# Gradient of a gated mix of attention and S4 convolution: early loads between the stages, another memory layout in the S4 loop, and the parameter gradients moved ahead of the last weight-gradient sweep

## The chip, the cores and the metric

The kernel runs on one core of a Trainium2 chip. The metric is the device time of one execution in microseconds (us), taken as the median over several runs. TensorE (PE) multiplies matrices, VectorE (DVE), ScalarE (ACT) and GpSimd (POOL) work on tiles, and SyncE (SP) issues most of the transfers (DMAs). SP, ACT and POOL each feed a DMA queue of their own, and all queues are served by the core's 16 DMA engines. Each engine runs its instructions in the order in which they are written into its program, and an instruction that waits holds up those behind it.

## What is computed

The kernel returns the output and all parameter gradients of this function, for a given gradient of the output:

```python
g = sigmoid((x * gate_w).sum(-1, keepdims=True))
a = attention(x, wqkv, wo)              # 32 heads of 18, S = 2048, D = 576
b = s4_conv(x, A, B, C, log_dt, Dskip)  # 576 channels, 128 states each
out = g * a + (1 - g) * b
...
out, vjp = jax.vjp(f, x, wqkv, wo, A_re, A_im, B_re, B_im, C_re, C_im, log_dt, Dskip, gate_w)
grads = vjp(grad_out)
```

The S4 kernel is K[d, l] = Re sum over n of C[d, n] · exp(dt[d]·A[d, n]·l) · dt[d]·B[d, n]. The convolution of every channel with its K, and the gradients through it, are computed in blocks of 128 positions: within a block by a Toeplitz matrix, and between the 16 blocks by a scan over states.

## The kernel before, in words

All work is in one function, `build`, in four stages.

**First stage** (to about 193 us). The projections, the gate and the S4 parameters are computed and written to HBM: `QKV_d`, `dO_d`, `par_d`, and reordered copies of x and of the output gradient (`xb_d`, `gyb_d`, `xr_d`, `gyr_d`).

**Attention, forward and backward** (to about 2190 us). The work of every four heads and 512 queries is a unit of 32 steps, and the backward rows follow the forward rows by `OFF` = 39 steps, so that ACT's two kinds of exponentials (`PT`, L799, and `eb`, L804), DVE's `ds` (L809) and PE's products interleave. The order on all five engines is written out by hand. After the last forward step (`NTOT`) a tail of 39 steps has only backward work, from about 2106 to 2178 us. On the way PE transposes some tiles into a PSUM tile `turn_p`, and DVE copies them out (L563: `dsT`, `dOaT`). The sums of dv and dk are kept in f32 accumulators; the last addition writes a bf16 tile `gb` (L612, L649), which a DMA transpose turns into `gT` (L532), POOL packs (`dtk`) and a DMA writes to `dqkv_d`. Beside this POOL computes the basis `E_d` of the S4 stage.

**S4 stage** (to about 2726 us), 18 blocks of 32 channels, in these steps for a block b:

- `m_load`: loads `xs` (1 MB) and `gyp`; `m_part`: products `psM` on PE, copied by ACT to `mst` and written to `Md_d`; `m_skw`: read back from `Md_d` along diagonals (`skw`); `m_sum` and `m_fin`: summed on PE (`misc`) and put into `RX`.
- `load_en`: loads the basis in two halves `E1n` of 1 MB; `turn_e`: PE transposes them (`etp`), ACT copies them out as `E1e`.
- `load_rx`, `prep_rx`: loads `RXn` for two blocks, and makes `RX` of it with three ACT operations.
- `uv`: products of `E1e` and `RX` on PE (`uvp`), copied by ACT to `UV`.
- `scan`: 15 dependent steps on DVE over `HG`, the first of which is a copy (L993) that marks the start of a block below. `casts`, `rw1`, `rw2`: the scan's results for PE (`hR`, `gR`, `Rw`).
- `k0`: one column of K into `Kp_d`; `t0_load`: the Toeplitz tile `T0w` (1 MB) out of it; `t0` and `ybp`: products into `yp`, copied to `yd` and every second block written to `yd_d`.
- `pairs1`, `pairs2`, `sums`: products on DVE, summed on PE into `SS` for the parameter gradients.

The order on PE, ACT, DVE and POOL is that of the program text; only SP's order is chosen by the scheduler. A lead-in brings blocks 0 to 2 on their way, and the loop runs block i together with uv of block i+1 and the m steps and loads of blocks i+2 and i+3:

```python
                m_load(0)
                load_rx(0)
                load_en(0, 0)
                load_par(0)
                load_en(0, 1)
                m_load(1)
                m_part(0, 0)
...
                for i in range(-1, NBLK):
```

**Final stage.** `x_tok`, then four column ranges of the token gradients (`load_dq(0)` to `load_dq(3)` into `dq_all`) are loaded, and between them the parameters (`zz`, `Wri`, `dt_b`, `prm5`). PE makes dWqkv in 20 groups of 16 matmuls (`ps_dwq`: four column ranges `FQS`, five row chunks each). DVE computes the parameter gradients in a chain (L1202 and around) that ends in six tiles `opad`; PE transposes each (`opt`, L1278), ACT copies (`obo`, L1280), and POOL issues the output DMAs (L1281, L1283). Two short products `fr` give the gradient of log_dt. Then a loop over 16 token tiles makes the two outputs of token shape (`ps_a`, `ps_dx`), with the transposed tiles `OT4` (L1342, per four tiles) and `dqT` (L1352, each tile) and `y_b`, `dxr_b` from `yd_d`. `pgw` and `ps_dwo` come last.

Memory comes from pools that open and close with the stages. By default, the first use of memory that an earlier pool had waits for everything that used the earlier pool there. With `reuse_waits="tile"` it waits for the users of those tiles alone that lay at the same addresses.

Of the kernel before, what the change touches and what calls it, by code (L numbers as in the profile page):

```python
# [20 lines left out]
def build(tc, aps, dbg_aps=None, stages=("s1", "attn", "post", "s4", "final")):  # L21
# [40 lines left out]
    with ExitStack() as gctx:  # L62
# [366 lines left out]
        if "attn" in stages:  # L429
# [5 lines left out]
            with ExitStack() as ctx:  # L435
                ctx.enter_context(tc.manual_schedule(engines={mybir.EngineType.PE, mybir.EngineType.Activation, mybir.EngineType.DVE, mybir.EngineType.Pool, mybir.EngineType.SP}))
                ga = ctx.enter_context(tc.tile_pool(name="ga", bufs=2))
                ptp = ctx.enter_context(tc.tile_pool(name="ptp", bufs=41))
                work = ctx.enter_context(tc.tile_pool(name="awork", bufs=2))
                apsp = ctx.enter_context(tc.tile_pool(name="aps", bufs=1, space=bass.MemoryType.PSUM))  # L440
# [85 lines left out]
                def grad_tile():  # L526
                    return work.tile([P, KB], BF, tag="gb", bufs=2, name="gb")

                def store_grad(gb, g, which, t0):
                    c0 = which * D + g * 4 * DH  # L530
                    gT = work.tile([P, TPQ, 4, HP], BF, tag="gT", bufs=2, name="gT")
# [21 lines left out]
                def turn(tiles, outs):  # L553
# [6 lines left out]
                    def ev():  # L560
                        x = 0
                        for n, o_ in outs:
                            nc.vector.tensor_copy(o_(), pt_[:, x:x + n])  # L563
                            x += n
# [32 lines left out]
                def dv_half(g, b, kq, h, acc):  # L597
# [6 lines left out]
                    def ev():  # L604
# [5 lines left out]
                        if b == NQ - 1:  # L610
                            o_ = DKV[("v", g, kq)] = grad_tile()
# [21 lines left out]
                def dk_half(g, b, kq, h, acc):  # L633
# [7 lines left out]
                    def ev():  # L641
# [5 lines left out]
                        if b == NQ - 1:  # L647
                            o_ = DKV[("k", g, kq)] = grad_tile()
# [179 lines left out]
        if "s4" in stages:  # L828
# [3 lines left out]
            s4c_cm = tc.tile_pool(name="s4c", bufs=1)  # L832
# [7 lines left out]
            with ExitStack() as ctx:  # L840
                pc = ctx.enter_context(tc.tile_pool(name="s4l", bufs=1))
                pw = ctx.enter_context(tc.tile_pool(name="s4lw", bufs=1))
                pps = ctx.enter_context(tc.tile_pool(name="s4lps", bufs=1, space=bass.MemoryType.PSUM))
# [13 lines left out]
                for u in range(2):  # L857
                    g_u = pc.tile([P, 2 * SUB, CB], BF, name=f"gyp{u}")
                    nc.vector.memset(g_u[:, SUB:2 * SUB, :], 0.0)
                    gyp2.append(g_u)  # L860
# [18 lines left out]
                def load_rx(xb):  # L879
                    d0 = xb * XB  # L880
                    RXn = pw.tile([P, 2 * NB, XB], BF, tag="RXn", bufs=1, name="RXn")
                    nc.sync.dma_start(RXn[:, 0:NB, :], xr_d[:, :, d0:d0 + XB])
                    nc.sync.dma_start(RXn[:, NB:2 * NB, :], gyr_d[:, :, d0:d0 + XB])
                    RXs[xb] = [RXn, None]
# [14 lines left out]
                def m_load(b):  # L899
                    xs = xss[b] = pw.tile([P, NSUB, SUB, CB], BF, tag="xs", bufs=2, name="xs")  # L900
                    src = bass.AP(tensor=xb_d.tensor, offset=xb_d[b:b + 1, 0:1, 0:1].offset,
                                  ap=[[XR * SUB * CB, NB], [SUB * CB, NSUB], [1, NSUB * SUB * CB]])
                    nc.sync.dma_start(xs.rearrange("p e t c -> p (e t c)"), src)
                    nc.sync.dma_start(gyp2[b % 2][:, 0:SUB, :].rearrange("p t c -> p (t c)"), gyb_d[b])
# [19 lines left out]
                def m_skw(b):  # L924
                    skw = skws[b] = pw.tile([P, CB // 8, P], F32, tag="skw", name="skw")
# [24 lines left out]
                def turn_e(b, h, q0, q1):  # L950

                    B_ = blk(b)
                    if q0 == 0:
                        B_["E"][h] = pw.tile([P, GS, 2, N], BF, tag="E1e", bufs=2, name="E1e")
                    En, E_ = B_["En"][h], B_["E"][h]
                    for q in range(q0, q1):
# [4 lines left out]
                        nc.scalar.copy(E_[:, 4 * q:4 * q + 4], pt_)  # L961

                def load_par(b):
                    par = blk(b)["par"] = pw.tile([P, 12, CB], F32, tag="par", bufs=2, name="par")
                    nc.sync.dma_start(par, par_d[:, 0:12, b * CB:(b + 1) * CB])

                def load_en(b, h):
                    dG = b * CB + h * GS
                    En = blk(b)["En"][h] = pw.tile([P, GS, 2, P], BF, tag="E1n", bufs=6, name="E1n")
                    nc.sync.dma_start(En, E_d[:, dG:dG + GS])  # L970
# [80 lines left out]
                def ybp(b, h):  # L1051
# [12 lines left out]
                    if h == 1 and b % 2 == 1:  # L1064
                        x0 = (b // 2) * XB
                        nc.sync.dma_start(yd_d.rearrange("p a b d -> p (a b) d")[:, :, x0:x0 + XB], yd.rearrange("p a b d -> p (a b) d"))
# [48 lines left out]

                m_load(0)
                load_rx(0)
                load_en(0, 0)
                load_par(0)
                load_en(0, 1)  # L1120
                m_load(1)
                m_part(0, 0)
                m_part(0, 1)
                m_skw(0)
                turn_e(0, 0, 0, 2)
                prep_rx(0)
                turn_e(0, 0, 2, 4)
                m_sum(0)
                m_fin(0)
                k0(0)  # L1130
                t0_load(0)
                load_en(1, 0)
                load_en(1, 1)
                load_en(2, 0)
                load_en(2, 1)
                m_part(1, 0)
                m_part(1, 1)
                for i in range(-1, NBLK):
                    cur = i >= 0
# [3 lines left out]
                    if sb is not None:  # L1143
# [21 lines left out]
                    if sb is not None:  # L1165
                        prep_rx(sb)
                    if cur:
# [21 lines left out]
        if "final" in stages and "s4" in stages:  # L1189
# [14 lines left out]
            with ExitStack() as ctx:  # L1204
                pb = ctx.enter_context(tc.tile_pool(name="pb", bufs=1))
                pps = ctx.enter_context(tc.tile_pool(name="pps", bufs=2, space=bass.MemoryType.PSUM))
                pbw = ctx.enter_context(tc.tile_pool(name="pbw", bufs=2))
# [14 lines left out]
                with ExitStack() as actx:  # L1222
                    pf = actx.enter_context(tc.tile_pool(name="pf", bufs=1))
# [220 lines left out]
```

## Time and profile before

| | us |
|---|---|
| median of three runs | 2948.57 (2947.92 to 2948.86) |
| span of the profiled execution | 2936.2 |
| attention, first PE product to last | 203 to 2184 |
| first scan of the S4 stage, block 0 / block 1 / block 2 | 2234.66 / 2262.93 / 2289.82 |
| last product of the loop on PE | 2724.0 |
| `ps_dwq` | 2741.05 to 2805.2 |
| token loop, from the first `ps_a` | 2824.37 to 2908.8 |
| `pgw` and `ps_dwo` | 2908.8 to 2932.6 |

The page gives the busy share of each engine in 40 slices of the span. A windows view gives for a stretch of time the busy microseconds and, in brackets, the number of instructions of each engine, then the clock that PE was granted, the busy share of the DMA engines, and what they moved. A timeline gives the start and duration of each instruction, its engine and line, what it writes and reads, and in square brackets how long its engine had been idle and what released it. SPq and ACTq are the issues of DMAs by these engines.

### The profile page before, as it was taken

To read this page: it belongs to the slowest core of one execution; us is meant where nothing else is said; L and a number is where in the kernel's file an instruction comes from. 1 tells how busy PE (TensorE), PEld (TensorE's weight loads), DVE (VectorE), ACT (ScalarE), POOL (GpSimd) and SP (SyncE) were. 2 spreads that over 40 slices of the span, in tenths; PEclk is the share of its full clock that TensorE was granted. 3 is DMA by queue.
4 is the path that set the end of the run, shared out by engine and by line. 5 is a ranking of instruction groups with operands and counts; after the bars stand their busy time and mean duration, and the time that the engine had idled before them with its cause. 6 is when DMAs were issued, how large, how long until landed. Compare 5 with 4: busy or idle time off the path is not lost.

```text
span 2936.2 us, 69578 instructions
## 1 busy us (share of the span) xinstructions
PE 2460.4 (84%) x27132; PEld 1182.8 (40%) x27132; DVE 2357.5 (80%) x4147; ACT 2375.9 (81%) x2792; POOL 1606.4 (55%) x2653
## 2 busy tenths in 40 slices
PE   4768988988888898898898888888866888885779
PEld 2432333332333233233333323333225878885457
DVE  4445998898898899799899989889864999999634
ACT  2449999999999999899999989999836877785111
POOL 1028888888788788787888778878210000000010
PEclk8877999999999999899999999999977888888889
DMA  8855899999989989988998998998789888882985
GB/s 224 163 152 106 157 157 171 158 164 160 170 153 167 170 153 168 168 150 161 164 168 152 166 157 156 161 173 146 130 141 263 216 222 228 214 221 63 268 195 131
DMA packets 1293343, 499.99 MB, mean 170 GB/s; under 512 B 1187774, under 2 KB 1263136, under 8 KB 1283796
## 3 DMA queue, kind: packets, MB, share of 16 engines
q1 hardware_dynamic: 1264500, 434.91, 77.1%
q0 software_dynamic: 20624, 53.26, 7.4%
q10 hardware_dynamic: 7888, 7.38, 0.8%
q8 instruction: 212, 3.47, 0.5%
q14 instruction: 119, 0.97, 0.1%
HBM read 144.48 MB, written 99.69 MB: 83 GB/s over the span
## 4 chain that ended last, share of the span: by engine, by line
ACT 34%; DVE 24%; PE 21%; DMA 8%; issue 7%; POOL 4%; SPq 3%; ACTq 0%; DVEq 0%; POOLq 0%
ACT eb L804 20%; ACT PT L799 13%; PE ps_P L30 7%; DVE ds L809 7%; DVE tz L999 4%; DVE tz L1002 3%; DVE HG L1003 2%; PE accV L30 2%; PE turn_p L558 2%; PE ps_dx L30 2%; DMA gT<-gb 2%; PE ps_dwq L30 2%; PE accK L30 2%; DVE pq L1069 1%; POOL et L358 1%
## 5 line engine op out<-in xcount | busy, mean ns | idle before, releaser
L809 DVE TENSOR_TENSOR ds<-ps_P,PT 128x512 bf16<-128x512 f32 x2048 | 1310.5, 682 | 123.2 <-PE ps_P L30 82.5
L804 ACT ACTIVATE eb<-ps_P 128x1024 bf16<-128x1024 f32 x1024 | 1098.7, 1073 | 72.1 <-PE ps_P L30 71.0
L799 ACT ACTIVATE PT<-ps_P 128x1024 bf16<-128x1024 f32 x1024 | 1102.0, 1079 | 3.2 <-PE ps_P L30 2.3
L30 PE MATMUL ps_P<-dOaT,VaT_g 32*128 32x512 bf16 x2048 | 580.6, 389 | 31.2 <-DVE ds L809 16.1
L358 POOL TENSOR_TENSOR et<-eG,eT 128x448 f32<-128x448 f32 x576 | 542.1, 961 | 10.7
L30 PE MATMUL ps_P<-QaT_g,KaT_g 32*128 32x512 bf16 x2048 | 412.9, 395 | 145.2 <-ACT PT L799 129.5
L30 PE MATMUL ps_P<-KaT_g,QaT_g 32*128 32x512 bf16 x2048 | 407.5, 391 | 2.2 <-ACT eb L804 1.6
L30 PEld LDWEIGHTS <-KaT_g 32*128 32x128 bf16 x2048 | 147.2, 91 | 480.1 <-issue 465.5
L358 POOL TENSOR_TENSOR Eo<-et,et 128x448 bf16<-128x448 f32 x288 | 327.0, 1136 | 20.8
L1105 POOL TENSOR_TENSOR SS<-m 128x96 f32<-128x96 f32 x18 | 8.9, 497 | 518.3 <-ACT m L1103 518.3
L30 PEld LDWEIGHTS <-QaT_g 32*128 32x128 bf16 x2048 | 115.9, 91 | 286.7 <-issue 265.1
L30 PE MATMUL accO<-PT,Vtok_g 128*32 128x512 bf16 x2048 | 213.2, 403 | 0.0
L30 PE MATMUL accV<-eb,dOa 128*32 128x512 bf16 x2048 | 184.6, 394 | 28.3 <-ACT eb L804 28.3
L30 PE MATMUL accK<-dsT,Qtok_g 128*32 128x256 bf16 x4096 | 166.6, 285 | 4.0 <-DMA dsT<-ds 2.4
L558 PE MATMUL turn_p<-ident_bf,ds 128*128 128x128 bf16 x1664 | 137.3, 226 | 32.1 <-DVE gb L630 31.2
L30 PE MATMUL accQ<-ds,Ktok_g 128*32 128x512 bf16 x2048 | 159.4, 389 | 2.5 <-DVE gb L612 2.1
L961 ACT COPY E1e<-etp 128x1024 bf16<-128x1024 bf16 x144 | 135.7, 1037 | 23.3 <-PE etp L960 17.7
L563 DVE COPY dsT<-turn_p 128x1024 bf16<-128x1024 bf16 (+1 forms) x224 | 143.7, 641 | 3.8 <-PE turn_p L558 3.8
L30 PEld LDWEIGHTS <-Vtok_g 128*32 128x32 bf16 x2048 | 53.6, 93 | 224.9 <-issue 224.1
L558 PEld LDWEIGHTS <-ds 128*128 128x128 bf16 x1664 | 100.4, 100 | 80.4 <-issue 80.4
L30 PEld LDWEIGHTS <-E1n 128*128 128x128 bf16 x2304 | 96.7, 109 | 87.2 <-issue 86.8
L30 PE MATMUL yp<-Rw,E1n 128*128 128x30 bf16 x1152 | 67.7, 232 | 68.7 <-DVE Rw L1024 54.2
(247 smaller groups left out, 3710.1 us busy)
## 6 DMA issues: line engine op xcount, KB each, us to landing
E_d<-Eo POOLq DMA_DIRECT2D x144, 256.0 KB, 3.7
E1n<-E_d SPq DMA_DIRECT2D x36, 1024.0 KB
xs<-xb_d SPq DMA_DIRECT2D x18, 1024.0 KB
T0w<-Kp_d SPq DMA_DIRECT2D x18, 1024.0 KB
Md_d<-mst SPq DMA_DIRECT2D x36, 288.0 KB
dsT<-ds SPq DMA_TRANSPOSE x512
dqkv_d<-dtk POOLq DMA_DIRECT2D x96, 72.0 KB, 4.4
QKV_d<-stg SPq DMA_DIRECT2D x12, 504.0 KB
```

The costliest lines, as they stand in the source:

```text
L30: return nc.tensor.matmul(out, lhsT=lhsT, rhs=rhs, start=start, stop=stop, **kw)
L358: nc.gpsimd.tensor_tensor(out, a, b, op=op)
L558: nc.tensor.transpose(pt_[:, x, qb, :], t_[:, qb * P:(qb + 1) * P], ident_bf)
L563: nc.vector.tensor_copy(o_(), pt_[:, x:x + n])
L799: nc.scalar.activation(U["PT"][i, j // 2], ps, ACT.Exp)
L804: nc.scalar.activation(e, ps, ACT.Exp)
L809: nc.vector.tensor_tensor(U["ds"][i][:, j, :], ps, U["PT"][i, j // 2][:, j % 2, :], op=A.mult)
L961: nc.scalar.copy(E_[:, 4 * q:4 * q + 4], pt_)
L999: nc.vector.tensor_tensor(tz, HG[:, :, k - 1, :].unsqueeze(1).to_broadcast([P, 2, 4, CB]), ZZ, op=A.mult)
L1002: nc.vector.tensor_tensor(t0v, t0v, UVk[:, :, :, k, :], op=A.add)
L1003: nc.vector.tensor_tensor(HG[:, :, k, :].rearrange("p (r s) c -> p r s c", s=2), t0v, t1v[:, ::-1], op=A.add)
L1069: nc.vector.tensor_tensor(o.rearrange("p a b n c -> p a b (n c)"), a_.rearrange("p b n c -> p b (n c)").unsqueeze(1).to_broadcast([P, 2, 2 ...
```

## The change

- **Pools.** The pools of attention, S4 stage and final stage get `reuse_waits="tile"`. The loop's tiles are spread over more pools in another order (`pl_` for the loads, `ple` for `E1n`, `pw` for the rest), so that they lie at other addresses.
- **Attention.** The last dv and dk sums are written as bf16 into the accumulators themselves, so that `gb` needs one buffer, and `gT` has three. In the steps from `NTOT` to `NTOT + OFF` the copies out of `turn_p` are made by ACT instead of DVE.
- **Lead-in.** It is written anew, with SP's order fixed too. The loads of block 0 (`xs`, `gyp`, first `E1n`, `RXn`, `par`) are issued by ACT. The `E1e` copies of block 0 are made by DVE. `m_part` of block 2 and its `m_skw` move from the lead-in into the loop's first pass.
- **End of the loop.** The last `yd_d` write is issued by ACT.
- **Final stage.** The first three of the four `ps_dwq` sweeps stand ahead of the parameter gradients as before; the fourth stands behind them.

```diff
-                ga = ctx.enter_context(tc.tile_pool(name="ga", bufs=2))
+                ga = ctx.enter_context(tc.tile_pool(name="ga", reuse_waits="tile", bufs=2))
...
-                            nc.vector.tensor_copy(o_(), pt_[:, x:x + n])
+                            (nc.scalar.copy if NTOT <= now[0] < NTOT + OFF else nc.vector.tensor_copy)(o_(), pt_[:, x:x + n])
...
-                            o_ = DKV[("v", g, kq)] = grad_tile()
+                            o_ = DKV[("v", g, kq)] = in_place(a_)
...
-                pc = ctx.enter_context(tc.tile_pool(name="s4l", bufs=1))
-                pw = ctx.enter_context(tc.tile_pool(name="s4lw", bufs=1))
+                pc = ctx.enter_context(tc.tile_pool(name="s4l", reuse_waits="tile", bufs=1))
+                pl_ = ctx.enter_context(tc.tile_pool(name="s4ld", reuse_waits="tile", bufs=1))
+                ple = ctx.enter_context(tc.tile_pool(name="s4le", reuse_waits="tile", bufs=1))
+                pw = ctx.enter_context(tc.tile_pool(name="s4lw", reuse_waits="tile", bufs=1))
...
-                        nc.sync.dma_start(yd_d.rearrange(...
+                        (act_dma if b == NBLK - 1 else nc.sync.dma_start)(yd_d.rearrange(...
...
-                m_load(0)
-                load_rx(0)
-                load_en(0, 0)
-                load_par(0)
-                load_en(0, 1)
-                m_load(1)
-                m_part(0, 0)
...
-                for i in range(-1, NBLK):
+                with tc.manual_schedule(engines={mybir.EngineType.SP}):
+                    m_load(0, act_dma)
+                    load_en(0, 0, act_dma)
+                    load_rx(0, act_dma)
+                    load_par(0, act_dma)
+                    m_part(0, 0)
+                    m_part(0, 1)
+                    m_skw(0)
+                    load_en(0, 1)
+                    prep_rx(0)
+                    turn_e(0, 0, 0, 4, dve_copy)
+                    m_load(1)
+                    m_sum(0)
+                    m_fin(0)
+                    load_en(1, 0)
+                    uv(0, 0)
+                    turn_e(0, 1, 0, 4, dve_copy)
+                    uv(0, 1)
+                    k0(0)
+                    load_par(1)
+                    prep_rx(1)
+                    m_part(1, 0)
+                    m_part(1, 1)
+                    load_en(1, 1)
+                    t0_load(0)
+                    m_skw(1)
+                    turn_e(1, 0, 0, 4)
+                    m_load(2)
+                    m_sum(1)
+                    m_fin(1)
+                    load_en(2, 0)
+                    load_en(2, 1)
+                for i in range(NBLK):
...
+                    if i == 0:
+                        m_part(2, 0)
+                        m_part(2, 1)
+                        m_skw(2)
...
-                pb = ctx.enter_context(tc.tile_pool(name="pb", bufs=1))
+                pb = ctx.enter_context(tc.tile_pool(name="pb", reuse_waits="tile", bufs=1))
...
-                    for f0, fn, c0 in FQS:
+                    def dwq(f0, fn, c0):
...
+                    for q in FQS[0:3]:
+                        dwq(*q)
...
+                    dwq(*FQS[3])
```

## The prediction

> **What bounds the kernel now.** I read the page first, for where no engine is full, then windows, then the timeline of the places found. All times are from one profiled execution of 2936.2 us.
>
> ```profile
> DVE  4445998898898899799899989889864999999634
> ...
> DMA  8855899999989989988998998998789888882985
> GB/s 224 163 152 106 157 157 171 158 164 160 170 153 167 170 153 168 168 150 161 164 168 152 166 157 156 161 173 146 130 141 263 216 222 228 214 221 63 268 195 131
> ```
>
> A slice is 73.4 us. Attention fills the slices up to about 2178 us and the S4 loop those from 2235 to 2721. Between them lies one slice in which DVE is at 4 tenths, and where the loop ends one in which traffic falls to 63 GB/s. Windows around these places (PE, PE weight loads, DVE, ACT, POOL busy; clock; DMA share; GB/s):
>
> ```profile
> 2200.00:2260.00 60.00, 35.66 (x554) 31.59 (x555) 22.16 (x49) 36.15 (x54) 0.00 (x0) 0.70 0.99 254
> 2500.00:2580.00 80.00, 70.32 (x1164) 66.72 (x1164) 74.97 (x157) 62.63 (x95) 2.78 (x6) 0.87 0.86 219
> 2660.00:2716.00 56.00, 28.46 (x512) 27.72 (x512) 52.61 (x107) 25.04 (x40) 1.94 (x4) 0.77 0.14 33
> 2716.00:2741.00 25.00, 7.26 (x122) 7.19 (x122) 6.33 (x8) 1.65 (x3) 4.52 (x12) 0.64 0.71 209
> 2806.00:2829.00 23.00, 6.22 (x35) 3.49 (x35) 3.48 (x6) 3.76 (x6) 8.59 (x13) 0.58 0.53 128
> ```
>
> Inside the loop DVE is the bound (74.97 of 80). In the lead-in the DMA engines are (0.99), with every compute engine idle part of the time. Just before the loop ends they rest (0.14), and then PE works 7 of 25 us waiting for them. At 2806 nobody is busy: small dependent steps. The timeline names the waits (start, duration, instruction, idle time before it and its releaser):
>
> ```profile
> 2192.35 0.58 SPq L903 DMA_DIRECT2D xs<-xb_d  x1
> ...
> 2199.98 2.10 PE L30 MATMUL psM<-xs,gyp 128*32 128x128 bf16 x32 [15.72 <-DMA xs<-xb_d]
> ...
> 2203.78 2.94 SPq L917 DMA_DIRECT2D Md_d<-mst  x2
> ...
> 2234.66 0.23 DVE L993 CAST HG<-UV 128x128 f32<-128x128 bf16 x1 [48.88 <-DMA Md_d<-mst]
> ...
> 2726.82 9.25 SPq L1228 DMA_DIRECT2D dq_all<-dqkv_d  x2
> ...
> 2741.05 13.77 PE L30 MATMUL ps_dwq<-dq_all,x_tok_b 128*128 128x426 bf16 x64 [17.03 <-DMA dq_all<-dqkv_d]
> ...
> 2746.50 0.76 DVE L1202 TENSOR_TENSOR fta<-zz,SS 128x576 f32<-128x576 f32 x1 [18.79 <-DMA zz<-par_d]
> ...
> 2824.37 2.56 PE L30 MATMUL ps_a<-wo_sb,OT 128*128 128x288 bf16 x10 [8.64 <-DMA OT<-O_tok]
> ```
>
> Each "idle before" is a stage start held by a load, and each load was issued only after the whole stage before had let go of its memory.
>
> **The skill.** "DMA: Bandwidth & Descriptors", section "Queues, rings and completion order": SP and ACT each own one row of rings on the same 16 engines, and an engine alternates between rows that have work. So a load issued by ACT needn't stand behind SP's and shares bandwidth with them. The page of before has 434.91 MB on SP's queue and only 7.38 on ACT's, so it can't confirm this. Its section "Why small descriptors are slow (HBM only)" agrees with the last yd_d write: 512 KB in 128-byte pieces took 5.28 us, 99 GB/s against the lead-in's 254. "TensorE: Matmul & The Clock Gate", Part 1, has an idle array fall to half clock; the trace agrees (0.50 in 2178 to 2200), so a shorter idle stretch saves some slow matmuls too. I count that at nothing, as these stretches still hold waits.
>
> **The change, part by part.** The orders and waits come from the built programs of both kernels; durations from the trace of before.
>
> A, attention's start. The last write of the first stage is issued at 190.89 and the first KaT load, which waits for it, at 193.23. With waits by tile it waits for older writes only: 193.23 − 191.34 (that issue's end) = 1.9 of which I take 1.8 (0 to 2.3). POOL's basis work starts earlier too, off the path.
>
> B, attention's tail, 2108 to 2178. DVE is busy 62.59 of 70 us, ACT 38.78. Nine turn copies (0.41 to 0.69 us on DVE, sum about 5) move to ACT, where a 1024-wide copy takes 1.04. PE, in order, waits both for exps (ACT) and for ds (DVE); a copy ahead of an exp delays it. Between −2 and +4, I take +1.5. In-place dv and dk sums cost nothing: the same DVE operation writes elsewhere.
>
> C, lead-in. xs, gyp, E1n, RXn and par of block 0 go to ACT's queue right after the last exp (2175.39 + 1.02) and wait by tile. ACT has nothing else until 2201, so six issues (0.4 to 0.6 each, one longer) delay nobody but these. xs can start at 2176.5 instead of 2192.35, and psM follows the last accK matmul (2184.3) instead of 2199.98. From psM to the Md_d write was 3.8 us: 2188. That write took 12.72 us to land, behind loads in its own queue; now SP's queue is empty ahead of it, and I take 3 to 5: 2192. Then as in before: skw 2.7, m_sum 2.4, casts about 1: 2198. The two uv halves follow without k0 and psM(1) between (1.84 + 2.17 before), paced by E1n(0,1), 1 MB issued at about 2195 and landed at about 2200, its turn (2 on PE) and UV copies (2.2): the first scan at about 2209 (2207 to 2212), 25 earlier than 2234.66. DVE's eight E1e copies, 8 × 0.69 (its 1024-wide copy at 2181.61), lie in its idle time.
>
> But the gain that counts is that of block 1, since blocks follow at 26.95 us (2289.82 − 2262.93, and the same between later ones). Block 1's earliest is 2209 + 27 = 2236. Its own chain: k0(0) ends about 2209, psM(1) 2211, mst behind three RX casts of block 1 on ACT (4.1) 2215; Md(1) shares the queue with E1n(1,1) and T0w, 2 MB, so about 10 to land: 2225; skw 2.7, m_sum 2.4, cast 1, k0 1.84, uv 2, E1e copies on ACT 3.8, second uv and UV copies 4.2: 2243, plus the hR casts' share of ACT, 2245 (2237 to 2251). Before it was 2262.9: gain 18 (12 to 25). Loads needed by then are about 10 MB, 39 us at 254 GB/s from 2176.5: 2216, so bandwidth alone isn't last. Blocks 2 and on keep their order.
>
> D, end of loop. x_tok (2304 KB) now waits for tiles that block 16's work lets go and is issued some 40 us earlier, into the stretch with DMA share 0.14: free. dq_all(0) still waits for block 17's last yp matmul (2716.75 + 3.56 = 2720.3), so the layout gives it no block, only the 6.5 us from 2720.3 to 2726.82. Its 1708 KB with yd_d's 512 KB need 8.5 us at 266 GB/s (the rate of 2741 to 2806), plus issue and landing about 1.7: ps_dwq at 2730.5 instead of 2741.05. Gain 10.5 (9 to 13). yd_d on ACT's queue removes its 0.56 us issue on SP from in front.
>
> E, final stage. Three of four ps_dwq sweeps (240 matmuls) take 64.1 − 80 × 0.187 = 49.2: 2779.7. Meanwhile DVE's parameter chain starts when zz lands: zz stays behind dq_all(1) on SP, 6.9 earlier than 2746.50, so 2739.6, and its 40.6 us (2746.50 to 2787.09) end at 2780.2. It is thus ready just as PE reaches the 30 opt transposes, which now lie between matmuls of the last sweep: 80 × 0.187 = 15.0 plus 3.5 of transposes and fr gives 2798.2; the waits for output DMAs (2806 to 2818 before) are filled by matmuls, I add 0.3 (up to 3). SP's queue ahead of OT4 (wqkvT, O_tok, go_all, rowb) ended at 2789.5 before and moves earlier with dq_all, so OT4, dxr and dqT, no longer held by the last POOL output, are there at about 2798: ps_a at 2798.5 instead of 2824.34, 25.8, of which D is 10.5 and E 15.3. PE waited for dqT 1.40 and 7.11 us after that; with loads further ahead I credit 2 (0 to 4). The rest (16 tiles, pgw, ps_dwo: 111.9 us) is unchanged. E: 17.3 (13 to 22).
>
> Sum: 1.8 + 1.5 + 18 + 10.5 + 17.3 = 49.1; span 2887. The timed median stands 12.4 above the profile's span, so 2948.57 − 49 = **2900**. Ends summed: 32 and 66.
>
> **Rivals.**
> 1. Lead-in traffic becomes the wait. Its window already had share 0.99; if Md(1) needs the 12.7 us that Md(0) took, and E1n(2,·) and T0w get in front, block 1 starts at 2251 or later: C gives 12 or less. For it: 0.99. Against: loads start 16 us earlier. With some of E lost too: 2908 to 2919.
> 2. Final loads hold ps_a. O_tok and go_all (2304 KB each) and wqkvT stand on SP's queue behind dq_all(2), ahead of OT4, and the share was already 0.91 in 2741 to 2806. If the SP queue keeps its old times, E is about 4, not 17: 2913.
> 3. Everything lands first: block 1 follows block 0 at once (2236, C 26), D 13, E 20: 62, so 2886.
> 4. Slower: the loop's period grows. Block 2's m_part sits inside block 0 and the load pools are rearranged, so traffic may mix with small pieces as in the last stage (2829 to 2909: share 1.00 at 217 GB/s). A block moves 26.95 × 219 = 5.9 MB; at 254 GB/s that is 23.2 us, hidden below DVE's 26.95. Below 219 DMA sets the period, and from 29.7 us (5.9 MB at 199 GB/s) 18 blocks take back the 49: slower beyond. Against it: the same transfers as before.
> 5. It doesn't do what it says: dq_all(0) indeed isn't freed a block early, priced in D already; the other parts don't depend on it.
>
> **Chances.** Forecast 0.60 (gain 38 to 58, so 2890 to 2911), rival 1 0.18, rival 2 0.06, rival 3 0.11, rival 4 0.03, no difference 0.02. The range for 8 in 10 reaches into 1, 2 and 3: 2884 to 2918. About 0.2% (5.9 us) can be told from no change: faster 0.95, same 0.02, slower 0.03.
>
> **What would show it.** Right: psM within 2 us of the last accK; the first scan near 2207, block 1 some 35 us later, then 26.95 each; x_tok issued before the loop's end, dq_all at its last yp; ps_dwq 10 us after; ps_a right behind the last sweep. Wrong: Md(0) again over 10 us in flight; a period above 27; PE idle ahead of opt or ps_a by more than 3 us; more than 2 us lost in attention's tail.

## The result, and the profile after

The changed kernel takes 2912.52 us (median of four runs, 2908.25 to 2918.88) against 2948.24 of before (four runs): a ratio of 0.9884, with a 95% interval of 0.9863 to 0.9904. That is 35.7 us less. The forecast was 49 less, with a range of 31 to 65. A second series gave 2913.64 and a ratio of 0.9882 (0.9854 to 0.9910). The profile fell on the longest of the first four executions (2918.88, span 2917.2), that of the kernel before on a short one (2937.9, span 2936.2), so stages are compared below by their own lengths, and over several profiles where there are some.

The page of the changed kernel, busy tenths in slices of 72.9 us:

```profile
DVE  4445998899898899899999989989865899999744
...
DMA  8764889999999989988998998998789888885795
GB/s 223 165 163 97 157 160 169 158 160 167 160 160 164 175 153 164 174 152 159 168 173 154 165 161 155 160 179 149 132 138 218 219 221 219 228 218 152 189 257 120
```

The slice of the lead-in has DVE at 5 tenths instead of 4, and the one with 63 GB/s at the loop's end is gone: 152 now. The windows show how far each place was mended (columns as before: PE, PE weight loads, DVE, ACT, POOL; clock; DMA share; GB/s):

```profile
2174.00:2214.00 40.00, 18.91 (x225) 14.63 (x224) 8.04 (x18) 9.29 (x15) 4.97 (x12) 0.64 1.01 190
2214.00:2253.00 39.00, 22.59 (x376) 20.41 (x375) 25.07 (x52) 20.78 (x33) 0.00 (x0) 0.69 0.92 224
2253.00:2290.00 37.00, 27.11 (x434) 25.31 (x432) 24.99 (x53) 22.58 (x35) 3.02 (x2) 0.82 0.74 201
...
2500.00:2580.00 80.00, 69.56 (x1164) 65.89 (x1164) 75.00 (x156) 62.44 (x94) 2.49 (x6) 0.87 0.84 215
2660.00:2716.00 56.00, 32.04 (x535) 31.29 (x533) 52.61 (x106) 27.33 (x43) 1.67 (x4) 0.74 0.27 77
2716.00:2730.00 14.00, 7.34 (x124) 6.92 (x124) 6.38 (x8) 1.65 (x3) 3.66 (x11) 0.74 0.54 160
```

The loop's steady part is the same (75.00 of 80 on DVE). The end of the loop now carries x_tok (77 GB/s instead of 33), and the gap behind it is 14 us long instead of 25. The first three lines are the surprise. Block 0's first scan comes at 2214.8, block 1's at 2253.01, and block 2's at 2290.46: DVE is busy 25 of 39 us and 25 of 37 in the two blocks that should already run at the loop's pace. The timeline, instruction by instruction (start, duration, and in brackets the idle time of the engine and its releaser):

```profile
2189.35 1.04 PE L30 MATMUL accK<-dsT,Qtok_g 128*32 128x256 bf16 x16 [9.77 <-DMA dsT<-ds]
2190.18 2.18 PE L30 MATMUL psM<-xs,gyp 128*32 128x128 bf16 x32
...
2214.77 0.23 DVE L999 CAST HG<-UV 128x128 f32<-128x128 bf16 x1 [1.61 <-ACT UV L992]
...
2235.47 8.62 SPq L909 DMA_DIRECT2D xs<-xb_d  x1
2244.14 0.88 SPq L889 DMA_DIRECT2D RXn<-gyr_d  x1
...
2253.01 0.22 DVE L999 CAST HG<-UV 128x128 f32<-128x128 bf16 x1
...
2255.08 2.02 ACT L899 COPY RX<-RXn 128x1024 bf16<-128x1024 bf16 x1 [3.33 <-DMA RXn<-gyr_d]
...
2290.46 0.22 DVE L999 CAST HG<-UV 128x128 f32<-128x128 bf16 x1
...
2679.64 0.44 SPq L1231 DMA_DIRECT2D x_tok_b<-in_A_x_dram  x1
2721.61 2.62 SPq L1250 DMA_DIRECT2D dq_all<-dqkv_d  x2
...
2729.72 31.97 PE L30 MATMUL ps_dwq<-dq_all,x_tok_b 128*128 128x426 bf16 x160 [4.89 <-DMA dq_all<-dqkv_d]
...
2739.62 0.74 DVE L1224 TENSOR_TENSOR fta<-zz,SS 128x576 f32<-128x576 f32 x1
...
2784.71 0.69 ACT L1305 COPY obo<-opt 128x640 bf16<-128x640 bf16 x1 [3.62 <-DMA O_tok<-O_d]
...
2785.45 0.44 PE L1303 MATMUL opt<-ident_bf,opad 128*128 128x128 bf16 x5 [3.12 <-ACT obo L1305]
...
2803.84 1.40 PE L30 MATMUL ps_a<-wo_sb,OT 128*128 128x288 bf16 x10
```

In the kernel before, the last `accK` matmuls ran in one piece:

```profile
2182.36 1.90 PE L30 MATMUL accK<-dsT,Qtok_g 128*32 128x256 bf16 x32 [0.78 <-DVE dsT L563]
```

In the changed kernel the last dsT transpose holds PE for 9.8 us ahead of the last 16 of them. The second half of RXn for blocks 2 and 3 stands behind a load of xs that takes SP 8.6 us to issue, and block 2's RX copies wait for it. The end is as planned: x_tok 42 us ahead of the loop's end, dq_all at its last yp matmul, ps_a right behind the last sweep.

The 19.0 us between the two profiled spans, by stage. "Last accK" is the first of the last 32 accK matmuls, the point at which attention's work on PE ends if nothing is late.

| stage | before | after | difference |
|---|---|---|---|
| start to first attention product | 203.5 | 201.9 | −1.6 |
| first product to last accK | 1978.9 | 1976.7 | −2.2 |
| last accK to first scan of block 0 | 52.3 | 36.2 | −16.1 |
| the same to block 1 | 80.6 | 74.5 | −6.1 |
| **the same to block 2** | 107.5 | 111.9 | **+4.4** |
| first scan of block 2 to that of block 17 | 404.3 | 404.8 | +0.5 |
| first scan of block 17 to ps_dwq | 46.9 | 34.4 | −12.5 |
| ps_dwq to ps_a | 83.3 | 74.1 | −9.2 |
| ps_a to the end | 111.8 | 113.3 | +1.5 |

So in the profiles the new lead-in gains 16 us at block 0 and has lost 4 by block 2, and the gain lies in the end of the loop and the final stage. The second row hides two changes that nearly cancel: the body of attention (first to last forward product) is 10.4 us shorter, 1890.1 instead of 1900.4, and the tail behind it 8.1 longer, 86.6 instead of 78.5.

The medians differ by 36 us where the profiled executions differ by 19: that of before lies about 10 below its median, that of the changed kernel 6 above. Two profiles don't tell which stage makes executions of one kernel differ, so the parts were run alone.

### The profile page after: what moved, and what is told of

Its sections match the earlier page's. It is cut to its first block, busy times and chain, and to the rows that moved or that the text cites. A ratio compares the mean times of both kernels' runs of the same rounds, so it can differ in the third digit from the quotient of the medians.

```text
span 2917.2 us, 69513 instructions
## 1 busy us (share of the span) xinstructions
PE 2484.6 (85%) x27132; PEld 1186.6 (41%) x27132; DVE 2359.3 (81%) x4146; ACT 2377.2 (81%) x2793; POOL 1610.9 (55%) x2653
## 4 chain that ended last, share of the span: by engine, by line
ACT 35%; DVE 23%; PE 23%; DMA 8%; issue 6%; SPq 3%; POOL 0%; ACTq 0%; DVEq 0%; POOLq 0%
ACT eb L808 21%; ACT PT L803 13%; PE ps_P L30 8%; DVE ds L813 7%; DVE tz L1005 3%; PE accV L30 3%; DMA dsT<-ds 2%; DVE tz L1008 2%; DVE HG L1009 2%; PE turn_p L562 2%; PE ps_dx L30 2%; PE accK L30 2%; PE accO L30 1%; DVE pq L1075 1%; DVE dvacc L616 1%
## 5 line engine op out<-in xcount | busy, mean ns | idle before, releaser
L30 PE MATMUL ps_P<-dOaT,VaT_g 32*128 32x512 bf16 x2048 | 587.6, 396 | 28.9 <-DVE ds L813 13.7
L30 PE MATMUL ps_P<-KaT_g,QaT_g 32*128 32x512 bf16 x2048 | 414.3, 397 | 1.2 <-ACT eb L808 0.6
L30 PE MATMUL accV<-eb,dOa 128*32 128x512 bf16 x2048 | 190.5, 405 | 26.6 <-ACT eb L808 25.7
L967 ACT COPY E1e<-etp 128x1024 bf16<-128x1024 bf16 x136 | 128.0, 1034 | 16.5 <-PE etp L966 16.4
L30 PEld LDWEIGHTS <-Qtok_g 128*32 128x32 bf16 x4096 | 88.9, 98 | 97.9 <-issue 64.9
L358 POOL TENSOR_TENSOR et<-eT 128x32 f32<-128x32 f32 (+3 forms) x288 | 116.1, 423 | 11.4
```

The source lines that it names most:

```text
L30: return nc.tensor.matmul(out, lhsT=lhsT, rhs=rhs, start=start, stop=stop, **kw)
L358: nc.gpsimd.tensor_tensor(out, a, b, op=op)
```

## The experiments

Four kernels ran together first, beside the kernel before (2939.45 us in that series). Each series has its own time of the kernel before, so results are compared by their ratio to it.

**The final stage alone.** The kernel before with the change's final stage:

```diff
-                pb = ctx.enter_context(tc.tile_pool(name="pb", bufs=1))
+                pb = ctx.enter_context(tc.tile_pool(name="pb", reuse_waits="tile", bufs=1))
...
+                    for q in FQS[0:3]:
+                        dwq(*q)
...
+                    dwq(*FQS[3])
```

> The kernel before with the final stage of the change alone (waits by tile in its pools, fourth weight-gradient sweep behind the parameter gradients); attention, lead-in and loop as before. My theory now, from the two profiles: the final stage is where nearly all of the measured gain lies (ps_dwq 12.5 us sooner after the last scan, ps_a 9.2 us sooner after ps_dwq, 1.5 us given back in the token loop), so about 20 us less than before, 2928. By the forecast's steps D and E: 27.8 less, 2920. A rival: the early x_tok load needs the loop's new memory layout, which is not in this kernel; then x_tok still goes after the loop and only the sweep's new place counts: 9 to 12 less, 2937.

Measured: 2924.18 us, ratio 0.9952 (0.9931 to 0.9974), 14 us less (7.6 to 20) where my theory had 20 and the forecast 28. In its profile ps_dwq follows block 17's first scan after 44.7 us (before 46.9, changed kernel 34.4), ps_a follows ps_dwq after 72.4 (83.3; 74.1), and the rest takes 107.9 (111.8; 113.3). The rival was right about x_tok, which went out only at 2718.10, behind the loop's last yp matmul: the early loads give 2 of their 12 us. The sweep's new place gives its whole gain without the new layout.

**All but the final stage.** The changed kernel with the final stage of before, its pools and its order:

```diff
-                pb = ctx.enter_context(tc.tile_pool(name="pb", reuse_waits="tile", bufs=1))
+                pb = ctx.enter_context(tc.tile_pool(name="pb", bufs=1))
...
-                    dwq(*FQS[3])
```

> The changed kernel with the final stage of before (pools that wait for the whole stage, parameter gradients behind all four sweeps); attention, lead-in and loop as changed. My theory: the lead-in's 20 us at block 0 are lost again by block 2, and what is left is attention's 3 to 4 us and what differs from execution to execution: 2938 to 2948. By the forecast's steps A, B and C: 21 less than before, 2927.

Measured: 2933.48 us, ratio 0.9986 (0.9967 to 1.0006): steps A, B and C together are not to be told from nothing, where the forecast had 21. My 2938 to 2948 and the forecast's 2927 were reckoned from 2948; against before in the same series the medians differ by 6 and the ratio by 4, which is inside my 0 to 10 and outside the 21 (the interval ends at 9.7). From block 17 to ps_dwq it takes 46.2: with the layout but pools that wait for the whole stage, step D's gain is gone as well. Layout and waits by tile each need the other. (`yd_d` on ACT's queue is in this kernel and not in the one above, so it isn't enough by itself.)

What the new final stage is worth can be read from what this kernel lacks: 0.9986 − 0.9884, or 30 us, give or take 8. Most of the change's 36 us is there.

**Block 0's loads on SP.**

```diff
-                    m_load(0, act_dma)
-                    load_en(0, 0, act_dma)
-                    load_rx(0, act_dma)
-                    load_par(0, act_dma)
+                    m_load(0)
+                    load_en(0, 0)
+                    load_rx(0)
+                    load_par(0)
```

> The changed kernel with block 0's loads issued by SP, behind the last transposes, instead of by ACT. My theory: ACT's loads share the DMA engines with attention's last dsT and gT transposes, and PE waits 9.8 us for dsT ahead of the last accK; here that wait is under 2 us and the last accK ends at about 2181 in the profile, not 2190; psM of block 0 starts within 3 us of where it started in the changed kernel, so the time is 0 to 6 us less, 2906 to 2912. The rival, that transposes were late for another reason: the wait of about 10 us stays, and psM comes 10 or more later: 2912 to 2925.

Measured: 2905.21 us, ratio 0.9891 (0.9871 to 0.9912), the same ratio as the changed kernel's. Its timeline, PE:

```profile
2178.45 1.90 PE L30 MATMUL accK<-dsT,Qtok_g 128*32 128x256 bf16 x32 [0.85 <-DVE dsT L567]
2184.14 2.14 PE L30 MATMUL psM<-xs,gyp 128*32 128x128 bf16 x32 [3.79 <-DMA gyp<-gyb_d]
```

All 32 accK matmuls run in one piece, and psM comes 5.7 us after their start instead of 11.6. So block 0's loads did hold up the transpose, as the Trainium skill would have it in "DMA: Bandwidth & Descriptors", section "Issuing engines are not separate DMA queues": all queues end on the same 16 engines and interleave. The edit changes queue and order at once (on SP the loads stand behind the last dsT), so it doesn't say which of the two counts. Block 0 starts 30.4 us after the last accK instead of 36.2, and psM 6 earlier where I expected 3 or less. But block 2's first scan still comes 110.0 us after the last accK (111.9), and no gain in time shows (the interval of each ratio is 6 us to either side, so a few could hide there). A wait of 10 us was removed on the way to block 0, and little or none of it arrived at block 2: something else sets that.

**Loads in the order of need.**

```diff
                     load_en(1, 0)
+                    load_en(1, 1)
                     uv(0, 0)
...
                     m_part(1, 1)
-                    load_en(1, 1)
+                    m_skw(1)
+                    load_rx(1)
                     t0_load(0)
-                    m_skw(1)
...
-                    if sb is not None and sb % 2 == 0:
+                    if sb is not None and sb % 2 == 0 and i > 0:
                         load_rx(sb // 2)
```

> The changed kernel with the lead-in's loads in the order of need: the second E1n half of block 1 directly behind its first, the read-back of block 1's diagonals ahead of T0w, and RXn of blocks 2 and 3 in the lead-in ahead of xs(2) and E1n of block 2 (in the changed kernel its second half stands behind two xs loads, is issued 23 us after the first half, and ACT waits 3.3 us for it with block 2's chain behind). My theory: block 1's first scan 3 to 6 us earlier and block 2's 5 to 12 earlier than in the changed kernel: 2900 to 2908. The rival, that the 24 MB moved between attention and block 2 set the time whatever their order: within 3 us of 2912.

Measured: 2895.29 us, ratio 0.9854 (0.9832 to 0.9876), about 10 below the 2905 that the changed kernel's ratio gives in this series (0.9884 × 2939.45). The intervals of the two ratios overlap a little, so the time alone would be weak evidence; the profile is not. The second half of RXn is issued 46 us after the last accK (2174.59) instead of 66, block 1's scan comes 63.8 us after it (74.5 in the changed kernel) and block 2's 99.4 (111.9), both earlier than I expected.

```profile
2220.68 1.55 SPq L889 DMA_DIRECT2D RXn<-gyr_d  x1
...
2273.97 0.22 DVE L999 CAST HG<-UV 128x128 f32<-128x128 bf16 x1
```

The wait for dsT is still there (8.15 us). The order of loads on SP was what held block 2, as my theory had it. Which of the three moves counts most was not tried; in the changed kernel's profile the chain to block 2 runs through RXn.

The second series asked about attention, and put the mended parts together (before: 2946.37).

**The changed kernel again.** No edit.

> The changed kernel once more, beside the others of this series. The one profile of it fell on its slowest execution (2918.88 against 2908 to 2913). My theory: attention's length differs from execution to execution by some 10 us in any kernel, and the wait of PE for the last dsT (9.8) and the distance from the last accK to block 2's first scan (111.9, against 107.5 before) are the same every time within 4 us. Ratio to before 0.986 to 0.991. The rival: the profile shows a bad case, and the distance is 100 or less here.

Measured: 0.9882, span 2911.2. The pause inside the last accK is 12.1 us from start to start (10.8 in the first profile), and block 2 comes 117.8 us after the last accK: 5.9 from the first profile, where I expected 4 at most, and away from the rival's 100. In four profiles with the new lead-in (this one, the first, and two more of this section) the distance is 111.9, 117.8, 115.7 and 115.1, in three with the old one 107.5, 108.5 and 110.4. The means are 115.1 and 108.8: the new lead-in costs 6.

**Attention's turn copies back on DVE.**

```diff
-                            (nc.scalar.copy if NTOT <= now[0] < NTOT + OFF else nc.vector.tensor_copy)(o_(), pt_[:, x:x + n])
+                            nc.vector.tensor_copy(o_(), pt_[:, x:x + n])
```

> The changed kernel with the copies out of turn_p in attention's tail back on DVE. In the profiles the tail (last forward product to the first half of the last accK) takes 74 to 79 us with the copies on DVE and 80 to 87 with them on ACT, with PE's granted clock near 1.0 for most of the former and 0.5 for most of the latter. My theory: the copies on ACT cost the tail 7 or so: here it takes 74 to 80 and the time is 4 to 9 us below the changed kernel's in this series. By the forecast's step B the copies on ACT gain 1.5: here 1 to 2 above. A rival, that the clock changes for another reason (waits by tile, in-place sums): tail 84 to 87 here too, and no difference in time.

Measured: 2912.49 us and 0.9882, the changed kernel's ratio to the last digit. My theory fell: the tail took 80.3 us with the copies on DVE and 79.9 with them on ACT in the same series. A small cost of the copies isn't excluded: over the nine profiles with the new attention pools the tail is 83.7 in the mean with the copies on ACT (six: 79.9 to 86.6) and 80.0 with them on DVE (three: 76.9 to 82.9). What remains is that the tail took 74 to 79 us (mean 76.5) in the three kernels with the old attention pools and 77 to 87 (mean 82.5) in those with the new ones, in-place sums alone being among the former, and that long tails go with a clock near 0.5 on PE. Which is cause and which is effect these runs don't say. (A low clock is no sign of idle time there: in 2123.9 to 2133.9 of the kernel before PE was busy 9.91 of 10 us at a granted clock of 0.50.)

**In-place sums alone.** The kernel before, with this only (the third `gT` buffer belongs to it, and was not tried apart):

```diff
-                    return work.tile([P, KB], BF, tag="gb", bufs=2, name="gb")
+                    return work.tile([P, KB], BF, tag="gb", bufs=1, name="gb")
...
-                    gT = work.tile([P, TPQ, 4, HP], BF, tag="gT", bufs=2, name="gT")
+                    gT = work.tile([P, TPQ, 4, HP], BF, tag="gT", bufs=3, name="gT")
...
-                            o_ = DKV[("v", g, kq)] = grad_tile()
+                            o_ = DKV[("v", g, kq)] = in_place(a_)
...
-                            o_ = DKV[("k", g, kq)] = grad_tile()
+                            o_ = DKV[("k", g, kq)] = in_place(a_)
```

> The kernel before with the in-place sums of dv and dk (one gb buffer, three of gT) and nothing else. In the profile of before DVE waits 34.4 us in seven waits for a gT transpose to let go of gb, and PE 30.4 us behind that; in the changed kernel both are gone, and PE waits 20 us for dsT instead of 2.4. My theory: attention's body is 5 to 10 us shorter by this alone, 2939 less 7 if before stands at 2939 again: ratio 0.996 to 0.999. The forecast's step B put it at nothing: 1.000 within 0.001.

Measured: 2933.70 us, ratio 0.9954 (0.9937 to 0.9971), 13.6 us less, more than my theory and far from nothing. The waits view says why. First the kernel before (engine, what waited, for what; us in total, how often, the longest), over attention's body:

```profile
DVE gb L630 <- DMA gT<-gb: 34.4, 7, 7.5
...
PE turn_p L558 <- DVE gb L630: 30.4, 7, 6.9
...
PE accK L30 <- DMA dsT<-ds: 2.4, 3, 1.6
```

At the end of each group of four heads the sums of dq, dk and dv all had to go through two gb buffers, each held by a transpose. DVE stood 34 us in seven waits, and PE 30 us behind it. With the in-place sums alone neither line is in the answer any more, and another has grown:

```profile
PE accK L30 <- DMA dsT<-ds: 20.4, 10, 5.4
```

On the same queue the dsT transposes are late instead; why, these views don't say. The body, first to last forward product, took 1891.6 us instead of 1900.4. The difference to 13.6 is within the interval and within what attention differs between executions.

**The mended parts together.** SP loads, order of need (RXn here behind xs(2) and its gyp), the copies on DVE, and block 2's part moved, with the loads of block 3 behind it:

```diff
                         turn_e(i + 1, 1, 0, 4)
+                    if i == 0:
+                        m_part(2, 0)
+                        m_part(2, 1)
+                        m_skw(2)
+                        m_load(3)
...
-                    if i == 0:
-                        m_part(2, 0)
-                        m_part(2, 1)
-                        m_skw(2)
```

> The changed kernel with what the runs so far point to: block 0's loads on SP behind the last transposes, the lead-in's loads in the order of need, block 2's m_part directly behind the second E1e turn of block 1 (ahead of hR on ACT) with xs(3) behind it, and the copies of attention's tail on DVE. My theory: 0 to 6 for the loads on SP, 10 for the order (measured 2895 against 2905), 6 to 9 for block 2, 4 to 9 for the tail: 17 to 30 below the changed kernel in this series; block 2's first scan 88 to 95 us after the last accK. The rival: traffic bounds the lead-in and one mended wait makes room for the next: no more than the 10 of the order.

Measured: 2889.55 us, ratio 0.9809 (0.9783 to 0.9834), 24 us below the changed kernel beside it, and 57 below the kernel before: the lowest ratio of all. The rival's limit of 10 lies at the edge of what was measured (the two ratios are 21 us apart, 10 to 33). Blocks 0, 1 and 2 start 30.5, 63.8 and 97.5 us after the last accK. The total came as expected, but not its parts: the tail took 82.9, so no gain of 4 to 9 shows there, and block 2 missed its 88 to 95, as its matmuls of m_sum still waited for the read-back of the diagonals.

```profile
2247.43 2.25 PE L30 MATMUL misc<-sel,skw 128*128 128x8 f32 x8 [5.49 <-DMA skw<-Md_d]
```

A last pair asked whether the new order in the lead-in was needed at all, and how much more order could give (before: 2945.80).

**The old order with waits by tile.** The changed kernel with the lead-in and loop of before:

```diff
-                with tc.manual_schedule(engines={mybir.EngineType.SP}):
-                    m_load(0, act_dma)
-                    load_en(0, 0, act_dma)
...
-                for i in range(NBLK):
-                    cur = True
+                m_load(0)
+                load_rx(0)
+                load_en(0, 0)
...
+                for i in range(-1, NBLK):
+                    cur = i >= 0
```

> The changed kernel with the lead-in and the loop's first passes in the order of before (SP's order left to the scheduler there, E1e copies on ACT, block 2's m_part in the lead-in); pools, memory layout, attention and final stage as changed. My theory: the new order loses 6 us at block 2 (115 from the last accK to its first scan in four profiles of it, against 107 to 110 in three of the old order), while waits by tile by themselves let the old order's first loads go earlier: 98 to 108 here, and a ratio to before of 0.982 to 0.987. By the forecast's step C the new order gains 18: then this is slower than the changed kernel, 0.992 to 0.995.

Measured: 2904.05 us, ratio 0.9853 (0.9829 to 0.9877), block 2 at 99.5 us after the last accK. As expected: with the layout, waits by tile alone give block 2 about 9 us over the kernel before (99.5 against 108.8), and the new order takes 16 away again (115.1). In time the difference to the changed kernel is 9 us, with an interval that reaches to nothing; the forecast's step C had this kernel slower (0.992 to 0.995), which is excluded.

**More order still.** Against the version of the mended parts:

```diff
                     load_en(1, 1)
+                    m_load(2)
                     uv(0, 0)
...
                     turn_e(1, 0, 0, 4)
-                    m_load(2)
                     load_rx(1)
...
                 for i in range(NBLK):
+                  with (tc.manual_schedule(engines={mybir.EngineType.SP}) if i == 0 else ExitStack()):
                     cur = True
```

> The version of the last series (0.9809) with xs(2) ahead of T0w and RXn in the lead-in, so that it is loaded while the DMA engines rest, and SP's order fixed for the loop's first pass too, with xs(3) behind block 2's read-back. In that version PE waited 1.5 us for gyp and 5.5 us for the diagonals of block 2. My theory: block 2's first scan 88 to 94 us after the last accK instead of 97.5, ratio 0.978 to 0.980. The rival, that traffic is the bound by now: 97 again and 0.981.

Measured: 2903.08 us, ratio 0.9841 (0.9810 to 0.9871); block 2 at 97.8, and 408.6 us from there to block 17 instead of 404. The expected gain didn't come. Whether traffic or the fixed order holds block 2 there wasn't tried further. From the last accK to block 2's first scan the DMA engines are 0.89 busy in the changed kernel (112 us), 0.86 in the version of the mended parts (97), 0.93 with the old order and waits by tile (99). So traffic may be near its limit there, and how much more order could give stays open.

## Why the prediction was right, and where it was wrong

The measured gain of 35.7 us lies in the forecast's range of 31 to 65, but low in it: outside the 38 to 58 to which the forecast itself gave its chance of 0.60, and inside the 2908 to 2919 us of its first rival. The terms did not hold alike.

**A, attention's start: right.** 1.8 forecast, 1.6 in the two profiles. The first KaT load now follows the issue of the last write at once (0.05 us; 1.9 before). Over all twelve profiles the first product comes at 201.2 to 204.6 us with the new pools and at 203.5 to 204.9 with the old, so a gain of this size is inside what executions differ by.

**B, attention: wrong in both parts.** The copies on ACT were to gain 1.5; they make no difference in time that shows (0.9882 with and without). The tail, for which the forecast allowed a loss of 2 at most, became 8.1 us longer in the two profiles and 6.0 in the means (82.5 against 76.5); the cause stays open. And the step that failed is the sentence that in-place sums cost nothing because "the same DVE operation writes elsewhere". The operation does take the same time; but the buffer that it no longer takes was one that DVE waited for, 34.4 us in all over attention's body, a wait that the forecast never counted. Alone it is worth 13.6 us (8.5 to 18.6).

**C, lead-in: wrong.** 18 forecast, a loss of 4 in the two profiles and of 6 over seven. Two sentences failed. "psM follows the last accK matmul (2184.3)" took the last dsT transpose to land as before, while 2 MB of loads were put into the same DMA engines beside it; PE waited 9.8 us. From psM on the chain to block 0 held (24.6 us; 24.7 forecast), but the wait, taken away, left the time where it was. The sentence that cost the gain is "Blocks 2 and on keep their order". I followed the chain to block 1 (2245 forecast, 2253.0 measured) and took a fixed 27 us per block from there. But in SP's queue the second half of RXn stands behind xs(2), xs(3) and E1n of block 2, and the mst copies of m_part(2) now stand on ACT behind the RX copies that wait for it; block 2 came 37.5 us after block 1. Rival 1 had the right place, traffic ahead of blocks 1 and 2, the right figure for block 1 (2251 or later) and the right range of time. Its cause was in part another: it took Md(1) to need 12.7 us, and the read-back behind Md(1) was issued 4.1 us after it; what came late was the read-back itself, with T0w in front as the rival had it, and PE waited for it until 2234.50. The runs show that the order of the traffic did much of it, since the order of need, with the same loads, gave 10 us. Even the best order reaches block 2 only 11 us earlier than the kernel before (97.5 against 108.8), not 18, so some of the rival's traffic may remain.

**D, end of the loop: right.** ps_dwq was forecast at 2730.5 and came at 2729.7, with block 17 1.2 later than in the kernel before; so 12.5 instead of 10.5 gained. dq_all was issued at the last yp matmul, as the working had it (rival 5's point), and x_tok 42 us before the end. The runs add that this gain needs both the layout and the waits by tile. That it exceeds 10.5 is the load itself: from the issue of dq_all to ps_dwq it took 8.1 us, not 10.2.

**E, final stage: right mechanism, size too large.** The first three sweeps were to end at 2779.7; the first opt transpose came at 2779.9. The parameter chain was to start at 2739.6 and did, at 2739.62. But from there to ps_a it took 23.9 us instead of 18.8. The term "I add 0.3 (up to 3)" for waits on output DMAs measured 4.2 (3.12 and 1.05 ahead of opt), one of the signs that the forecast had named for being wrong. Only the short wait comes from outputs that hold `obo`. Ahead of the long one ACT stood at the issue of an earlier `dwq_bf` output until 2784.19, when by the trace the load of O_tok had just landed; ACT's copy of `opt`, and PE behind it, came after that. The same releaser stands there in all nine profiles with the new final stage (1.1 to 4.2 us on ACT). Why an output's issue waits for that load, these runs don't say. The 2 us credited in the token loop didn't come in this profile (113.3 instead of 111.8), but in the mean they did: 109.7 over the nine with the new final stage (107.9 to 113.3) against 112.9 over three with the old one. So 9.2 and −1.5 in the two profiles where 17.3 stood.

Of the rivals, the third, everything in place first, fell with block 2. The fourth, a longer period, did not come: 404.8 us for 15 blocks against 404.3. The second fell for ps_a, which had its tiles when the last sweep ended, though one of the loads that it named, O_tok, did hold the steps before.

Three slips in the working move the sum by nothing that counts. 2289.82 − 2262.93 is 26.89, and 26.95 is the loop's mean (404.3 / 15). The line of 2234.66 names a write to Md_d, not a load. And the 99 GB/s of the last yd_d write are one transfer from issue to landing, set against 254 for many at once, so they don't single out its small pieces.

By parts: 13.6 (in-place sums) + 14.1 (final stage) + 10.3 (its early loads with the layout: 44.7 − 34.4) + 1.6 (start) − 6.3 (lead-in) − 6.0 (tail) = 27.3, against 35.7 measured. The sum mixes medians with distances in profiles, each uncertain by several us, so it shows the order of size and no more. Grouped as the runs measured it, steps A, B and C, forecast at 21, gave 4 (−2 to 10), and D and E, forecast at 28, gave about 30 by the difference of ratios and 20 in the two profiles. That the total stayed in the range is in part luck: the in-place sums, priced at nothing, made up for the lead-in and the tail. If they are worth as much in the changed kernel as alone, the gain without them would be about 22, below the range.

## What to carry to other kernels

An earlier start of a pipeline is worth what the first block of its steady state gains, not the first block: follow the queues, entry by entry, as far as the block from which the period is fixed. An edit of buffers is priced from the waits for the buffer it spares, not from the operation that it changes. And where a visible wait of 10 us goes away and the time stays, look for the queue entry that releases the next one; here the order of loads on one queue was worth about 10 us, and a second queue nothing that shows.

## What the runs showed of the hardware that was not expected

- Three loads of 2176 KB in all (xs, gyp and E1n), issued by ACT about when SP issued the last dsT transpose, stretched it: PE waited 7.6 to 11.0 us for it in the five profiles with these loads on ACT, and not at all in the four that had the new memory layout and the loads on SP, behind that transpose.
- Lead-in traffic reached share 1.01 at only 190 GB/s while transposes and small packets were among it (9168 of 11597 under 512 bytes, in 2174 to 2214), against 254 at 0.99 in the lead-in of before (11446 of 17654). The share alone doesn't tell how much more could be moved.
- A load of xs took SP 8.6 us to issue (the others of this stretch 0.5 to 0.7) with five loads of 1 MB issued in the 12 us before it, and everything behind it on SP waited that long. It took 7.6 to 8.6 at this place in all six profiles with the new lead-in and this load there.
